# A fused attention and GLU kernel: where its PSUM accumulators lie, when its LayerNorm runs, and how its last sums are added

## The chip, the cores and the metric

The kernel runs on one core of a Trainium2 chip. The core has five engines with their own in-order instruction queues: TensorE (PE, matrix products; loading its weights is shown as PEld), VectorE (DVE), ScalarE (ACT), GpSimd (POOL) and SyncE (SP, which here only issues DMA transfers). ACT and POOL issue DMA transfers too. Products are accumulated in PSUM, a small memory of eight banks that PE writes and DVE and ACT read; everything else lies in SBUF or in DRAM.

The metric is the device time of one execution in microseconds, median over runs of the same kernel. Less is better.

## The reference

The input is one sequence of 2048 tokens with 576 features. Two layers follow each other, each with a residual:

```python
h  = x + A(layernorm(x))     # attention: 32 heads of 18; each token sees 8 keys, 2 apart
h2 = h + B(layernorm(h))     # GLU: (sigmoid(x @ w_gate) * (x @ w_up)) @ w_down, 4608 hidden

# A
qkv = x @ wqkv                                   # [2048, 1728]
idx = pos[:, None] - 2 * arange(8)[None, :]      # the window; negative positions are masked
logits = einsum("bhsd,bhswd->bhsw", q, k[idx]) * 18 ** -0.5
o = einsum("bhsw,bhswd->bhsd", softmax(logits), v[idx]) @ wo
```

All data are fp32.

## The kernel before, in words

**Blocks.** The tokens are split by parity (a window steps by 2, so even tokens see only even ones) and by half, into four blocks of 512 tokens, each of 4 sub-blocks of 128. Each fp32 operand is split into a high part, which ACT rounds to fp32r (L105), and a low part, which DVE makes by subtraction (L106); a product is three matmuls: high by high, low by high, high by low. The last 64 features are packed twice into a fifth chunk (L108 to L110).

**QKV stage.** The 32 heads are four groups of 8. `qkv(b, g, ...)` (L355) makes q, k and v of one block and one group in four tiles of 14 matmuls with 432 columns (L151 to L154), which ACT copies out (L362), and three DMAs of ACT's queue write q, k and v to DRAM (L364 to L368). `ln1` (L327) normalizes a block by sub-blocks: statistics on DVE, the power on POOL, the scaling on ACT for blocks 1 to 3 (L131 to L133), then five transposes on PE (L140, L144) and a split (L105 to L110). `norm` runs a whole `ln1`, `heads` whole QKV products, in the order of L412 to L445. `attention` (L160) loads q and the windows of k and v again (SP) and works almost wholly on DVE (L173 to L207); it is a generator, and `step` lets it go on by a given number of steps after each tile of PE's work, so that it lies beside the matmuls. `att_all` (L376) has the order of its eight runs for blocks 0 and 1. When block 0 is done, `front` projects it, adds the residual, normalizes and transposes it for the MLP.

**MLP.** The 36 hidden tiles of 128 are gone through for the first pair of blocks, then for the second pair. The first 14 tiles of a pair are "std" items, for one block alone (`single`, L597); after that come "pair" items (`pair`, L623), for both blocks together by seven products of sums in place of eight, in three accumulators: b1 takes the products b00, t2, t1 and b11, b2 takes b10, b3 takes t3 and t4. Every product is six matmuls of 512 columns (L562), with two more for the packed rest (L569). Between the products, `between(0)` to `between(6)` let other work in: attention of blocks 2 and 3 in the first pair stage, down projections from a queue. In the second pair's pair stage, tiles 0 to 31 are projected down by seven products as well (`down_seven`, L722), whose results POOL's DMAs add up in DRAM (`hsev`); the last four tiles go by `down_tail` (L708), which adds to sums that `load_tails` (L1024) has loaded back, and writes the output.

**Weights.** One load per item (L516) brings the weights of one hidden tile into one of two buffers, two items ahead; `weights` (L528) splits them at a high priority.

**Order.** The kernel is written in a framework that sets the order on each engine by a simulated time line, from the order of the text and priorities (`high_priority`); each engine then works through its own list in that order, and waits are put in by the framework. `issue_after` holds instructions behind a given one. Memory is given out in pools: tiles of one tag share a number of buffers, and a new tile waits until a buffer is free.

## Time and profile before

| | us |
|---|---|
| time, median of 3 runs (lowest to highest) | 1610.49 (1609.51 to 1611.9) |
| the profiled execution by its own time | 1611.02 |
| its span in the profile | 1609.2 |
| PE busy | 1562.2 (97%) |
| DVE busy | 1253.3 (78%) |
| ACT busy | 881.9 (55%) |
| POOL busy | 191.4 (12%) |

The span runs from the first to the last recorded instruction; the time of the execution holds a little more. "Busy" is the time in which at least one instruction of an engine is on record. A matmul's record (0.39 us for 512 columns) is longer than the distance to the next one, as matmuls overlap, so short gaps between matmuls don't show as idle in full. The granted clock is the share of TensorE's full clock that it was given in a stretch. A row of a group reads: line, engine, operation, output and inputs with their sizes, count, busy us, mean ns of one, and the engine's idle time ahead of them with what ended it. In a row of the timeline, the first two numbers are start and length in us, and the bracket is the idle time ahead and what ended it. In a row of waits the three numbers are us in total, times, and the longest.

### The profile page before, as it was taken

How to read it: one execution, taken by the hardware profiler on the slowest of the kernel's cores; microseconds unless marked ns; L12 is line 12 of the kernel's file. 1: busy time of each engine (PE TensorE's matmuls, PEld its weight loads, DVE VectorE, ACT ScalarE, POOL GpSimd, SP SyncE). 2: the span in 40 equal slices, each digit the busy share in tenths (PEclk: the TensorE clock that was granted, in tenths of full speed). 3: DMA queues.
4: the chain of work that ended last, by engine and by line, in shares of the span. 5: the costliest groups of instructions: out<-in, count | busy, mean ns of one | idle time of the engine just before them, and what ended most of it. 6: DMA issues, size and time to landing. Idle time of an engine off the chain costs nothing.

```text
span 1609.2 us, 22432 instructions
## 1 busy us (share of the span) xinstructions
PE 1562.2 (97%) x8532; PEld 1381.6 (86%) x8532; DVE 1253.3 (78%) x1982; ACT 881.9 (55%) x1565; POOL 191.4 (12%) x230
## 2 busy tenths in 40 slices
PE   7899999999999999999999999999999999999998
PEld 6799988798788888888889987888888888888887
DVE  7989999648999999999635777777767777767755
ACT  6423235534455565555543344677767777667751
POOL 2000010001010010000011100121211221121210
PEclk9899999999999999999999999999999999999999
DMA  7446666654468565666685224699998999989992
GB/s 265 160 150 221 222 236 180 176 184 150 142 165 209 146 168 145 165 166 156 191 249 192 77 88 126 147 185 177 180 173 168 180 190 179 178 164 183 184 192 106
DMA packets 77788, 278.22 MB, mean 173 GB/s; under 512 B 8336, under 2 KB 14224, under 8 KB 76784
## 3 DMA queue, kind: packets, MB, share of 16 engines
q0 software_dynamic: 28944, 111.19, 39.0%
q1 hardware_dynamic: 40304, 143.70, 25.9%
q10 hardware_dynamic: 8432, 21.89, 3.6%
q8 instruction: 67, 1.10, 0.3%
q14 instruction: 41, 0.34, 0.1%
HBM read 145.88 MB, written 133.23 MB: 173 GB/s over the span
## 4 chain that ended last, share of the span: by engine, by line
PE 78%; DVE 12%; ACT 3%; DMA 3%; issue 3%; POOL 0%; SPq 0%; ACTq 0%; DVEq 0%; POOLq 0%
PE b L562 36%; PE dp L733 11%; PE dp L671 11%; PE acc L151 8%; PE b L569 7%; DVE pr L173 2%; DVE pr L199 2%; DVE w L106 1%; DVE lg L176 1%; PE bgp L151 1%; PE b L151 1%; DMA wg<-in_wmlp_dram 1%; DVE pr L204 1%; DVE s L582 1%; PE acc L154 1%
## 5 line engine op out<-in xcount | busy, mean ns | idle before, releaser
L562 PE MATMUL b<-tl,w 128*128 128x512 f32 x1728 | 443.2, 394 | 12.4 <-DVE s L582 6.6
L562 PEld LDWEIGHTS b<-tl,w 128*128 128x128 f32 x1728 | 314.1, 188 | 77.0 <-DVE s L582 6.7
L562 PE MATMUL b<-th,w 128*128 128x512 f32 x1380 | 360.3, 394 | 7.1 <-ACT s L645 5.7
L562 PEld LDWEIGHTS b<-th,w 128*128 128x128 f32 x1380 | 251.8, 188 | 58.8 <-ACT s L645 8.9
L105 ACT ACTIVATE w<-wg 128x640 fp32r<-128x640 f32 (+2 forms) x200 | 118.6, 597 | 168.4 <-PE b L569 108.7
L569 PE MATMUL b<-th,w 128*128 128x512 f32 x576 | 178.8, 390 | 0.0
L106 DVE TENSOR_TENSOR w<-wg,w 128x640 fp32r<-128x640 f32 (+2 forms) x200 | 129.2, 649 | 58.1 <-ACT w L105 55.0
L742 POOL DMA_DIRECT2D h<-ev x128 | 110.8, 868 | 442.8 <-ACT ev L739 428.1
L151 PE MATMUL acc<-qw,th 128*128 128x432 f32 x512 | 156.0, 366 | 0.8 <-ACT th L105 0.8
L739 ACT ACTIVATE ev<-dp 128x576 f32<-128x576 f32 x224 | 141.9, 649 | 24.6 <-PE dp L733 22.4
L569 PEld LDWEIGHTS b<-th,w 128*128 128x128 f32 x576 | 108.1, 188 | 22.9
L671 PE MATMUL dp<-d,h0h 128*128 128x288 f32 x640 | 123.4, 296 | 0.6 <-ACT stage L679 0.6
L671 PE MATMUL dp<-d,h1h 128*128 128x288 f32 x640 | 121.5, 295 | 0.5 <-DVE tail L681 0.5
L106 DVE TENSOR_TENSOR w<-tw,w 128x512 fp32r<-128x512 f32 x116 | 79.5, 686 | 45.4 <-ACT w L105 45.4
L671 PEld LDWEIGHTS dp<-d,h0h 128*128 128x128 f32 x640 | 101.8, 189 | 6.7 <-ACT stage L679 0.9
L671 PEld LDWEIGHTS dp<-d,h1h 128*128 128x128 f32 x640 | 100.6, 188 | 5.5 <-DVE tail L681 0.7
L151 PEld LDWEIGHTS acc<-qw,th 128*128 128x128 f32 x512 | 98.8, 193 | 5.8 <-ACT th L105 1.3
L151 PE MATMUL acc<-qw,tl 128*128 128x432 f32 x256 | 94.5, 369 | 0.4 <-DVE tl L106 0.4
L679 ACT ACTIVATE stage<-dp 128x576 f32<-128x576 f32 x112 | 71.1, 646 | 39.7 <-PE dp L671 39.2
L105 ACT ACTIVATE w<-tw 128x512 fp32r<-128x512 f32 x116 | 73.1, 630 | 30.0 <-PE b L562 23.4
L362 ACT ACTIVATE ev<-acc 128x432 f32<-128x432 f32 x64 | 33.8, 530 | 98.8 <-PE acc L154 98.8
L646 DVE TENSOR_TENSOR s<-s,b 128x512 f32<-128x512 f32 x58 | 39.6, 683 | 59.3 <-ACT s L645 59.3
(268 smaller groups left out, 2933.7 us busy)
## 6 DMA issues: line engine op xcount, KB each, us to landing
h<-ev POOLq DMA_DIRECT2D x96, 576.0 KB, 7.0
wg<-in_wmlp_dram SPq DMA_DIRECT2D x49, 928.0 KB, 5.7
h<-stage POOLq DMA_DIRECT2D x28, 1152.0 KB, 10.2
wg<-in_wmlp_dram SPq DMA_DIRECT2D x36, 640.0 KB, 4.8
kw<-k SPq DMA_DIRECT2D x16, 792.0 KB, 5.3
vw<-v SPq DMA_DIRECT2D x16, 792.0 KB, 4.8
wd<-in_wmlp_dram SPq DMA_DIRECT2D x18, 576.0 KB, 6.4
h<-ev POOLq DMA_DIRECT2D x32, 288.0 KB, 5.9
```

The lines of the kernel that those rows point to most:

```text
L105: act.activation(hi, src, AF.Copy)
L106: splits.append(dve.tensor_tensor(lo, src, f32(hi), ALU.subtract))
L151: pe.matmul(ps[:, :n], a[:, c, js], m[:, c], start=k == 0, stop=False)
L362: act.activation(ev[:, :, j], ps[:, :NQ].rearrange("p (t c) -> p t c", t=3), AF.Copy)
L562: pe.matmul(ps, wt[:, a, k0 + c], xx[:, m + c], start=first and k == 0, stop=k == 5, skip_group_check=True)
L569: pe.matmul(ps, wt[:, a, k0], xx[:, 4], start=False, stop=a == 1, skip_group_check=True)
L646: added[0] = dve.tensor_tensor(s3, s3, b3, ALU.add)
L671: pe.matmul(ps[:, i, :DH2], a[:, js], d[:, m, i * DH2:(i + 1) * DH2], start=k == 0, stop=k == n)
L679: act.activation(hv, ps, AF.Copy)
L733: pe.matmul(ps[:, i, :DH2], a[x][:, js], m[y], start=k in (0, 1, 3) and q == 0, stop=q == 2, skip_group_check=True)
L739: act.activation(hs[:, k % 2], ps[:, :, :DH2], AF.Copy)
L742: pool.dma_start(hsev[:, u, k0:k + 1], hs[:, :k + 1 - k0], accum_op=ALU.add, max_dma_last_dim=8 * D)
```

## The change

Four groups of edits.

- **Pair items:** the three accumulators change places from item to item (`turn`), and ACT copies b3 out right behind the t3 product, to which DVE later adds b1 (before: ACT copied b1 behind t1, and DVE added b3).
- **QKV stage:** `beside` puts the LayerNorm of a block, sub-block by sub-block, behind the tiles of a QKV product of another block. The order of the products and of the attention runs changes: block 0's four attention runs come first. QKV weights, and the two halves of the output weights, share three buffers (before: two, and an extra one). k and v lie in one DRAM tile per group and are written by one DMA; the zero pads likewise. The logits have two buffers.
- **MLP weights:** raw weights have three buffers and are loaded three items ahead; the first item's weights are split into a free operand buffer at the end of the QKV stage (`first_weights`).
- **End:** the stored sums are loaded into tiles of their own, and the second of two is added by an accumulating DMA of POOL. The first group of `down_tail` is copied out by ACT; in the last group DVE adds the stored sums and then the PSUM result. The scratch for the descriptors of POOL's DMAs is set to 8192.

```diff
@@ pads, attention
-            for s in (kscr, vscr):
-                a = s[e][g][0:LP, :]
-                sp.dma_start(..., zero)
+            a = kvscr[g][e]
+            sp.dma_start(..., zero.rearrange("p (t n) -> p t n", t=2))
-        lg = sm.tile([P, NS, W, HG], F32, bufs=1, name="lg")
+        lg = at.tile([P, NS, W, HG], F32, bufs=2, name="lg")
@@ ln1, qkv_w, qkv
-            pri = 2 * HI if b == 0 else HI if b > 1 else 0
+            pri = 2 * HI if b == 0 else HI
+    def qw_tile(name):
+        return saw.tile([P, 2, 5, NQ], F32R, tag="qw", bufs=3, name=name)
-        for t, s in ((1, kscr), (2, vscr)):
-            act.dma_start(s[e][g][r0:r0 + TB, :].rearrange("(p j) c -> p (j c)", p=P),
-                          ev[:, t].rearrange("p j c -> p (j c)"))
+        act.dma_start(kvscr[g][e][:, r0:r0 + TB].rearrange("t (p j) c -> p t (j c)", p=P),
+                      ev[:, 1:3].rearrange("p t j c -> p t (j c)"))
@@ att_all
-        for b, g in ((0, 0), (0, 1), (1, 0), (0, 2), (0, 3), (1, 1), (1, 2), (1, 3)):
+        for b, g in ((0, 0), (0, 1), (0, 2), (0, 3), (1, 0), (1, 1), (1, 2), (1, 3)):
@@ order of the QKV stage
+    def beside(b, xb, order, n):
+        gl = ln1(b, xb)
+        T.append(next(gl))
+        for a, g in order:
+            for _ in qkv(a, g, T[a], w[g]):
+                next(gl, END)
+                step(ag, n)
+        drain(gl)
...
-    heads(((0, 1),), w, 0)
-    norm(1, xb, 0)
+    beside(1, xb, ((0, 1),), 0)
+    w.append(qkv_w(2))
     pads(1)
+    pads(2)
+    heads(((0, 2),), w, 1)
     xb = load_x(2)
-    heads(((1, 0),), w, 1)
-    norm(2, xb, 1)
+    beside(2, xb, ((1, 0),), 2)
     xb = load_x(3)
-    heads(((2, 0),), w, 2)
-    norm(3, xb, 1)
+    beside(3, xb, ((2, 0),), 2)
     heads(((3, 0),), w, 2)
-    w.append(qkv_w(2))
-    pads(2)
-    heads(((1, 1), (0, 2), (2, 1), (3, 1)), w, 2)
     w.append(qkv_w(3))
     pads(3)
+    heads(((0, 3), (1, 1), (2, 1), (3, 1)), w, 2)
     h = load_x(0)
...
+    wos = [None, wo_w(1, wo_tile("wo1"))]
+    heads(((1, 2), (2, 2), (3, 2)), w, 2)
+    wos[0] = wo_w(0, wo_tile("wow"))
@@ weights of the first item, and their loads
+    def first_weights(ws):
+        t = th_tile().rearrange("p a (b n) -> p (a b) n", n=P)
...
+        split(w1[:, 0], w1[:, 1], r[:, 5:10])
+        split(w2[:, 0], w2[:, 1], r[:, 3:5])
+        split(w4[:, 0], w4[:, 1], r[:, 0:3])
     with tc.high_priority(HI):
         drain(fr)
+        first = first_weights(wg)
-        ws = gw.tile([P, WC], F32, bufs=2, name="wg")
+        ws = gr.tile([P, WC], F32, bufs=3, name="wg")
...
-            wc = weights(items[c + 1][0], wg, c + 1 < NF + NSTD)
-        if c + 2 < len(items):
-            wg = load_gu(items[c + 2][2], n=WC if c + 2 < NF + NSTD else GU)
+            wc = weights(items[c + 1][0], raws.pop(0), c + 1 < NF + NSTD)
+        if c + 3 < len(items):
+            raws.append(load_gu(items[c + 3][2], n=WC if c + 3 < NF + NSTD else GU))
@@ pair
-        b1, b2, b3 = b_tile(0), b_tile(1), b_tile(2)
+        b1, b2, b3 = (b_tile(i + turn[0]) for i in range(3))
+        turn[0] += 1
...
         prod(b3, X["s3"], w, "t3", True)
+        with tc.high_priority(HC):
+            act.activation(s3, b3, AF.Copy)
         between(3)
         prod(b1, X["s1"], w, "t1", False)
         rest(b1, X["a11"], w, "u4")
         with tc.high_priority(HC):
-            act.activation(s3, b1, AF.Copy)
-            added[0] = dve.tensor_tensor(s3, s3, b3, ALU.add)
+            added[0] = dve.tensor_tensor(s3, s3, b1, ALU.add)
@@ down_tail
+            if end:
+                with ExitStack() as ties:
+                    for i in over:
+                        ties.enter_context(tc.issue_after(i))
+                    dve.tensor_tensor(hv, hv, tile_j(more[b], j), ALU.add)
-            add_tile(hv, down_tile(seg, b - 2, j), False)
+            add_tile(hv, down_tile(seg, b - 2, j), not end)
@@ load_tails
-        yield from lag(7)
-        for a, m in adds:
-            with tc.issue_after(getattr(added[0], "ins", added[0])):
-                dve.tensor_tensor(a, a, m, ALU.add)
-            yield
+                        if i == 0:
+                            sp.dma_start(more[b][:, h], src)
+                        else:
+                            pool.dma_start(more[b][:, h], src, accum_op=ALU.add,
+                                           max_dma_last_dim=8 * D)
+        yield
@@ kernel
-    nc = _bacc.Bacc("TRN2", target_bir_lowering=False, num_devices=1)
+    nc = _bacc.Bacc("TRN2", target_bir_lowering=False, num_devices=1,
+                    dynamic_dma_scratch_size=8192)
```

`over` holds the last two split instructions of the last item, and each add of the last group: the adds of stored sums are held behind them on DVE.

## The prediction

> **What bounds the kernel now.** The first view is the page's busy table.

> ```profile
> span 1609.2 us, 22432 instructions
> PE 1562.2 (97%) x8532; PEld 1381.6 (86%) x8532; DVE 1253.3 (78%) x1982; ACT 881.9 (55%) x1565; POOL 191.4 (12%) x230
> ```

> TensorE (PE) sets the end. The change neither adds nor removes a matmul, so only time in which PE stands still or runs slowly can be won: 1609.2 - 1562.2 = 47 us of visible idle, and some more, because a matmul's record is longer than the interval to the next one. The second view shows where that time lies: busy time by stretch. The columns are the stretch, its length, busy us (and instructions) of PE, PEld, DVE, ACT, POOL, the granted TensorE clock, the DMA share and GB/s.

> ```profile
> 8.67:36.27 27.60, 27.20 (x132) 25.14 (x133) 21.46 (x78) 19.74 (x41) 6.83 (x12) 1.00 0.71 244
> 36.27:46.00 9.73, 6.72 (x34) 5.94 (x33) 8.65 (x14) 5.32 (x17) 1.33 (x3) 0.82 0.96 365
> 69.50:80.00 10.50, 7.25 (x27) 5.81 (x26) 10.27 (x14) 3.65 (x13) 0.00 (x0) 0.67 0.47 162
> 80.00:187.00 107.00, 107.00 (x548) 102.43 (x547) 96.80 (x105) 30.26 (x63) 0.92 (x1) 1.00 0.56 197
> 187.00:230.00 43.00, 41.73 (x264) 39.64 (x263) 41.58 (x71) 13.07 (x28) 4.77 (x6) 1.00 0.56 188
> 230.00:242.00 12.00, 9.02 (x36) 6.04 (x35) 11.93 (x13) 6.74 (x12) 0.00 (x0) 1.00 0.97 367
> 242.00:297.00 55.00, 54.98 (x292) 47.86 (x291) 49.54 (x66) 29.87 (x49) 3.17 (x3) 1.00 0.61 176
> 297.00:326.00 29.00, 25.54 (x134) 21.76 (x133) 16.36 (x24) 13.28 (x24) 2.75 (x3) 0.94 0.71 216
> 393.00:440.00 47.00, 42.67 (x203) 34.52 (x202) 43.48 (x60) 23.26 (x38) 1.24 (x1) 0.96 0.46 148
> 440.00:778.00 338.00, 330.52 (x1801) 288.00 (x1801) 322.18 (x435) 191.98 (x316) 29.46 (x29) 1.00 0.62 158
> 989.00:1020.00 31.00, 27.32 (x123) 21.32 (x122) 23.16 (x42) 16.79 (x29) 2.85 (x3) 1.00 0.63 157
> 1020.00:1560.00 540.00, 540.00 (x2924) 474.52 (x2924) 386.93 (x673) 385.16 (x680) 109.94 (x127) 1.00 0.92 176
> ```

> Three things are to be seen. From 1020 to 1560 us, the second pair stage, PE is never idle, so nothing can be won there. The losses lie at the two LayerNorms of the QKV stage (36 to 46 and 69.5 to 80 us, with the clock down to 0.82 and 0.67), at the start of the MLP (230 to 242), around 297 to 326, through the first pair stage (393 to 778), and at 989 to 1020. And from 187 to 297 and from 393 to 778 us VectorE (DVE) is about 95% busy with the attention that runs beside the matmuls: there PE can only become faster as far as DVE has room.

> **The change part by part.** The profiled execution took 1611.0 us by its own time, 1.8 us more than its span, and 0.5 us above the median of 1610.49. The sum is made against 1611.0.

> *LayerNorm between QKV tiles.* A full-rate QKV matmul takes 107.00 / 548 = 0.195 us (stretch 80 to 187).

> ```profile
> 36.27 0.60 PE L140 MATMUL mm<-ident,tok 128*128 128x128 f32 x4
> ...
> 36.82 0.60 PE L140 MATMUL mm<-ident,tok 128*128 128x128 f32 x4
> ...
> 41.67 0.86 PE L140 MATMUL mm<-ident,tok 128*128 128x128 f32 x4 [2.21 <-DVE tl L106]
> ```

> Five transposes take 0.55 us (36.27 to 36.82). The stretch from 36.27 holds 20 transposes and 14 QKV matmuls, 4 x 0.55 + 14 x 0.195 = 4.9 us of work in 9.73: 4.8 us are lost, some 3.0 to idleness and 1.8 to the clock. In the stretch from 69.5 at most 27 x 0.195 = 5.3 us of work stand in 10.5: 5.2 lost. Both times PE has emitted all transposes of a block and has nothing else until the first split of the block comes back. After the change, four tiles of another QKV product lie between them, so each split has 14 x 0.195 = 2.7 us of cover. I leave 0.5 us in each place: **4.3 and 4.7 us won**; if the splits are late, at least 0. The third LayerNorm and the output projection idle 43.00 - 41.73 = 1.3 us (187 to 230); block 0's attention is now first in DVE's list, one attention earlier: **0.5**, between 0 and 1.3.

> The cover needs ScalarE (ACT) to keep up.

> ```profile
> L362 ACT ACTIVATE ev<-acc 128x432 f32<-128x432 f32 x10 | 5.2, 524 | 11.9 <-PE acc L154 11.9
> L105 ACT ACTIVATE th<-mm 128x512 fp32r<-128x512 f32 x8 | 4.9, 612 | 1.6 <-PE mm L140 1.6
> L132 ACT ACTIVATE tok<-tok,rstd 128x576 f32<-128x576 f32 x6 | 4.3, 771 | 0.0
> L131 ACT ACTIVATE tok<-h,nm 128x576 f32<-128x576 f32 x4 | 2.8, 766 | 0.0
> L109 ACT ACTIVATE th<-acc 128x128 fp32r<-128x128 f32 x8 | 2.1, 300 | 0.0
> L133 ACT ACTIVATE tok<-tok 128x64 f32<-128x64 f32 x5 | 1.3, 267 | 0.0
> ```

> These groups of ACT (36.27 to 69.5 us; mean ns behind the busy us) give, per tile with its LayerNorm, 524 + 612 + 771 + 766 + 300 + 267 = 3240 ns. PE's turn is 2.73 + 0.55 = 3.28 us. It just fits. The third weight group, now split before block 0's third QKV product, adds to ACT at 8.67 to 36.27, where it is 19.74 of 27.6 us busy; there is room for five splits of 432 columns (each at most the 0.61 of the 512-column split above).

> [...] The granted clock falls here behind a gap of 2.2 us. [...]

> *First MLP weights split early.* In 230 to 242 us 36 matmuls at 0.225 us (1.35 us for six, below) are 8.1 us of work: 3.9 lost.

> ```profile
> 231.66 1.45 PE L562 MATMUL b<-tl,w 128*128 128x512 f32 x4 [1.25 <-ACT w L105]
> 233.75 1.20 PE L562 MATMUL b<-tl,w 128*128 128x512 f32 x4 [0.65 <-DVE w L106]
> ```

> The two waits for split weights go, as the splits now run under the last QKV product: **1.9**, between 0 (DVE is 11.93 of 12 us busy, so the same work may surface later) and 3.9.

> *Third weight buffer; attention's end.* The rows are PE, POOL, PE.

> ```profile
> 300.02 1.63 PE L562 MATMUL b<-tl,w 128*128 128x512 f32 x6 [1.35 <-DVE s L582]
> 307.27 0.75 POOL L210 DMA_DIRECT2D o<-kw  x1 [19.87 <-DVE kw L207]
> 320.85 0.66 PE L140 MATMUL b<-ident,oj 128*128 128x128 f32 x4 [1.65 <-DMA oj<-o]
> ```

> The wait at 300.02 follows a late weight load; loading one item further ahead removes it: **1.4**. But the last attention of block 1 leaves DVE only at 307.27, and PE already waits for its reload at 320.85. If PE comes 4.3 + 4.7 + 0.5 + 1.9 = 11.4 us earlier, DVE must do the same. Between 80 and 297 us DVE idles 10.2 + 1.4 + 0.1 + 5.5 = 17.2 us, much of it behind single waits in its queue, so it will gain part of that. I give back **4**; the ends are 11.4 (DVE gains nothing) and a further gain of 1.65 + 0.06 x 29 = 3.4 (this wait and its clock go too).

> *PSUM accumulators and the third eviction.* In a pair item, b1 took the last product and the next item's first, and product t4 could enter b3 only after ACT had copied b1 (L645) and DVE had added b3 (L646). Afterwards ACT copies b3 before the t1 product, and the next item starts in another accumulator.

> ```profile
> 1003.95 1.52 PE L562 MATMUL b<-tl,w 128*128 128x512 f32 x6
> 1005.30 0.61 PE L569 MATMUL b<-th,w 128*128 128x512 f32 x2
> 1006.61 1.65 PE L562 MATMUL b<-th,w 128*128 128x512 f32 x6 [0.69 <-ACT s L645]
> ```

> Six matmuls take 1.35 us, and t4 starts 1.31 us behind a group that needs 0.45: 0.86 us lost each time no down projection lies between. The weight loads' waits by window, 380 to 790, 985 to 1025 and 1560 to the end:

> ```profile
> PEld b L562 <- DVE s L582: 7.1, 7, 2.3
> PEld b L562 <- ACT s L645: 4.4, 4, 1.1
> PEld b L562 <- DVE s L646: 1.6, 2, 1.4
> ...
> PEld b L562 <- ACT s L645: 3.3, 3, 1.4
> PEld b L562 <- DVE s L651: 1.2, 1, 1.2
> ...
> PEld b L562 <- ACT s L645: 1.1, 1, 1.1
> PEld dp L671 <- DVE tail L681: 0.7, 1, 0.7
> ```

> In the first pair stage 7.1 + 4.4 + 1.6 = 13.1 us hang on these accumulators, plus 0.04 x 47 = 1.9 of clock: 15.0. DVE idles only 3.5 + 15.8 = 19.3 us in these 385, and would be 366 of 370 us busy if all came true. I take **9** (between 4, the waits for ACT alone, and 15). What is late next there is DVE's split of the hidden halves, which the change leaves alone. At 985 to 1025 DVE has room (23.16 of 31): **4** of 4.5, at least 3.

> *The end.* Stored sums are added into one tile by the DMA, and the last but one group of units is evicted by ACT, not added by DVE. L645's 1.1 and the 0.7 go. But these units no longer wait for the loaded sums, move up between the last pair items, and no longer lie between the last product and the last group; that one waits for its hidden split: multiply, ACT, about 0.7 + 0.6 us from DVE's and ACT's 128x512 rows, 1.2 after overlap. DVE gets two adds per unit.

> ```profile
> 1604.80 0.75 DVE L681 TENSOR_TENSOR tail<-tail,dp 128x576 f32<-128x576 f32 x1 [0.84 <-PE dp L671]
> ```

> DVE works 0.75 us per unit and idles 0.84 before it, so the second add of 0.75 fits, just. **0.6**, between -2.4 (both waits are paid) and 1.8. The merged k and v stores (16 ACT issues fewer), the merged pads (8 SP issues fewer), the second logits buffer and the output weights, which now wait for a QKV weight slot and are used only behind the last QKV product, I cost at nothing: they lie on ACT's and SP's queues and under PE's 107 busy us of 80 to 187; uncovered, they would delay attention, which is in the 4 above.

> Sum: 4.3 + 4.7 + 0.5 + 1.9 + 1.4 - 4 + 9 + 4 + 0.6 = 22.4 us. 1611.0 - 22.4 = **1588.6**.

> **The rivals.** *DVE is the bound.* What PE wins up to the reload comes back there in full, the 1.4 with it, and the first pair stage yields only 4: 4 + 4 + 0.6 = 8.6, so 1602.4. For it: the 95% busy stretches; against: 17.2 and 19.3 us idle in them.

> *All covers hold.* Every upper bound: 4.8 + 5.2 + 1.3 + 3.9 + 1.4 + 3.4 + 15 + 4.5 + 1.8 = 41.3, so 1569.7. For it: the second pair of blocks' attention is used late and may slip; against: DVE's queue is in order, and PE's splits stand in it.

> *LayerNorm is late at every turn: slower.* The transposes of three blocks now stand in PE's queue at 12 places, each in front of a QKV tile. If ACT's 3.24 us per turn stretch beyond PE's 3.28, each place waits. The whole sum then stands against 12 new waits: from 22.4 / 12 = 1.9 us per place on the gain is gone, and at the 2.2 us of today's wait on tl L106 it is 1611.0 - 22.4 + 26.4 = 1615. Against it: one late turn gives the next ones time.

> [...]

> *The order stays.* Engines follow the planner's simulated order, so the text's order may change little on PE: 1608 to 1614.

> **How the numbers follow.** Forecast 52% (own range 1580 to 1597), DVE bound 22% (1597 to 1607), all covers 13% (1569 to 1580), late LayerNorm 6%, POOL stall 1%, order stays 6%. A change within 0.2% (3.2 us) can't be told from none. Faster 0.87, same 0.06, slower 0.07. 1572 to 1606 leaves out 13% above, 2% at the upper edge of the DVE case and some 3% below.

> **What would show it.** Right: in the stretches 36 to 46 and 69 to 80 the clock stays at 1.00 and PE's waits for tl L106 are gone; waits for L645 and L646 vanish from PE's list, those for L582 shrink; DVE rises over 96% in the first pair stage. Wrong: new waits of the transposes on tok L133 or L135, a longer wait on oj, waits on hidden splits in place of L582, or clock dips elsewhere.

## The result and the profile after

| | before | after |
|---|---|---|
| time, median (lowest to highest), us | 1610.82 (4 runs) | 1584.03 (1582.09 to 1586.38; 4 runs) |
| ratio after / before, 95% interval | | 0.9835 (0.9819 to 0.9851) |
| the profiled execution, its span, us | 1611.02, 1609.2 | 1582.11, 1580.3 |

The kernel became 26.8 us faster. The forecast was 1588.6 with a range of 1572 to 1606, so the sign and nearly the size were right. The experiments below show that several terms of the sum were not.

The busy table of the kernel after, and the first row of its chain of work:

```profile
span 1580.3 us, 22467 instructions
PE 1548.5 (98%) x8532; PEld 1377.6 (87%) x8532; DVE 1257.2 (80%) x1979; ACT 879.8 (56%) x1573; POOL 192.4 (12%) x233
PE 87%; DVE 5%; issue 3%; DMA 2%; ACT 2%; POOL 0%; ACTq 0%; SPq 0%; DVEq 0%; POOLq 0%
```

PE's visible idle fell from 47.0 to 1580.3 - 1548.5 = 31.8 us. The stretches, with the columns that the prediction explains:

```profile
36.27:46.00 9.73, 8.57 (x49) 7.86 (x48) 9.21 (x26) 7.27 (x20) 3.04 (x4) 1.00 1.01 379
69.50:80.00 10.50, 10.35 (x58) 9.61 (x58) 10.24 (x13) 5.10 (x16) 0.00 (x0) 1.00 0.20 75
230.00:242.00 12.00, 6.55 (x22) 5.05 (x23) 11.97 (x12) 4.25 (x8) 0.00 (x0) 0.72 0.79 293
297.00:326.00 29.00, 28.07 (x159) 24.47 (x157) 14.86 (x25) 14.70 (x27) 3.92 (x4) 1.00 0.88 274
440.00:778.00 338.00, 337.60 (x1863) 298.44 (x1863) 319.38 (x433) 196.76 (x326) 28.58 (x27) 1.00 0.66 170
```

The clock at the two LayerNorms is back at 1.00 in this profile, and in the first pair stage PE is idle for 0.4 us where it was for 7.5. At 230 to 242 it became worse: 22 matmuls in place of 36. PE's longest waits of the whole run now (us in total, times, longest):

```profile
PE mm L141 <- DVE tok L136: 8.2, 1, 8.2
PE b L576 <- DVE w L106: 5.1, 1, 5.1
PE b L576 <- DVE s L598: 3.0, 5, 1.8
PE bgp L152 <- DVE hj L245: 1.9, 1, 1.9
PE mm L141 <- ACT tok L133: 1.7, 2, 1.3
PE mm L141 <- ACT th L109: 1.2, 1, 1.2
```

(The first is the wait for the first data. Line numbers moved: L562 is now L576, L569 L583, L582 L598, L671 L694, L681 L704.)

Because busy time hides short gaps (the record of a matmul of 512 columns lasts 0.39 us, the next one starts after 0.227), the two traces are compared by a **loss**: for each matmul, the time to the start of the next one, less the median of that time for matmuls of the same width (227 ns for 512 columns, 196 for 432, 132 for 288, 109 for 128, the same to 1 ns in the traces of before and after). It holds idle time and slow pitch alike. All losses of the kernel before sum to 67.9 us, of the kernel after to 39.7.

| stretch of each kernel's own time, us | before | after | won | forecast |
|---|---|---|---|---|
| 20 to 60, first LayerNorm between tiles | 5.9 | 1.4 | 4.5 | 4.3 |
| 60 to 92, second | 6.6 | 4.2 | 2.4 | 4.7 |
| 180 to 220, third, output projection | 2.2 | 2.3 | -0.1 | 0.5 |
| 220 to 240, start of the MLP | 4.0 | 7.5 | -3.5 | 1.9 |
| 240 to 440, std items, reload of attention | 15.9 | 8.9 | 6.9 | 1.4 - 4 |
| 440 to 790, first pair stage | 14.0 | 2.3 | 11.7 | 9 |
| 790 to 985, second pair's std items | 3.2 | 3.2 | 0.0 | - |
| 985 to 1020, start of the second pair stage | 5.5 | 0.2 | 5.2 | 4 |
| 1520 to the end | 3.3 | 2.3 | 0.9 | 0.6 |

### The profile page after: what moved, and what is told of

It is laid out like the page before. It is cut to its first block, busy times and chain, and to the rows that moved or that the text cites. A ratio compares the mean times of both kernels' runs of the same rounds, so it can differ in the third digit from the quotient of the medians.

```text
span 1580.3 us, 22467 instructions
## 1 busy us (share of the span) xinstructions
PE 1548.5 (98%) x8532; PEld 1377.6 (87%) x8532; DVE 1257.2 (80%) x1979; ACT 879.8 (56%) x1573; POOL 192.4 (12%) x233
## 3 DMA queue, kind: packets, MB, share of 16 engines
q1 hardware_dynamic: 39360, 141.93, 26.4%
## 4 chain that ended last, share of the span: by engine, by line
PE 87%; DVE 5%; issue 3%; DMA 2%; ACT 2%; POOL 0%; ACTq 0%; SPq 0%; DVEq 0%; POOLq 0%
PE b L576 42%; PE dp L694 14%; PE dp L766 11%; PE acc L152 8%; PE b L583 8%; PE bgp L152 1%; PE b L152 1%; DMA oj<-o 1%; PE acc L154 1%; PE acc L155 1%; DVE pr L174 1%; DVE w L106 1%; DMA ws<-in_wqkv_dram 1%; DVE lg L177 0%; DVE pr L200 0%
## 5 line engine op out<-in xcount | busy, mean ns | idle before, releaser
L576 PE MATMUL b<-tl,w 128*128 128x512 f32 x1716 | 454.3, 393 | 9.1 <-DVE w L106 5.1
L576 PEld LDWEIGHTS b<-tl,w 128*128 128x128 f32 x1716 | 310.7, 188 | 65.3 <-DVE w L106 5.8
L576 PE MATMUL b<-th,w 128*128 128x512 f32 x1368 | 357.2, 392 | 0.8 <-DVE s L672 0.6
L576 PEld LDWEIGHTS b<-th,w 128*128 128x128 f32 x1368 | 251.3, 188 | 48.7 <-DVE s L672 1.1
L772 ACT ACTIVATE ev<-dp 128x576 f32<-128x576 f32 x224 | 145.8, 651 | 114.8 <-PE dp L766 89.6
L583 PE MATMUL b<-th,w 128*128 128x512 f32 x572 | 179.7, 390 | 0.0
L105 ACT ACTIVATE w<-wg 128x640 fp32r<-128x640 f32 (+2 forms) x197 | 117.0, 596 | 93.2 <-PE b L583 60.0
L106 DVE TENSOR_TENSOR w<-wg,w 128x640 fp32r<-128x640 f32 (+2 forms) x197 | 127.4, 649 | 50.2 <-ACT w L105 49.9
L583 PEld LDWEIGHTS b<-th,w 128*128 128x128 f32 x572 | 107.1, 188 | 21.5
L694 PE MATMUL dp<-d,h1h 128*128 128x288 f32 x640 | 123.0, 295 | 0.0
L694 PE MATMUL dp<-d,h0h 128*128 128x288 f32 x640 | 122.5, 295 | 0.3 <-DVE tail L704 0.3
L106 DVE TENSOR_TENSOR w<-tw,w 128x512 fp32r<-128x512 f32 x116 | 79.5, 686 | 38.0 <-ACT w L105 37.9
L694 PEld LDWEIGHTS dp<-d,h0h 128*128 128x128 f32 x640 | 101.5, 188 | 6.3 <-DVE tail L704 0.6
L694 PEld LDWEIGHTS dp<-d,h1h 128*128 128x128 f32 x640 | 101.4, 188 | 5.4
L105 ACT ACTIVATE w<-tw 128x512 fp32r<-128x512 f32 x116 | 73.2, 631 | 53.7 <-PE b L576 41.5
L672 DVE TENSOR_TENSOR s<-s,b 128x512 f32<-128x512 f32 x58 | 39.6, 683 | 62.3 <-PE b L583 62.2
## 6 DMA issues: line engine op xcount, KB each, us to landing
h<-stage POOLq DMA_DIRECT2D x28, 1152.0 KB, 11.4
```

What stands on the lines that cost most here:

```text
L105: act.activation(hi, src, AF.Copy)
L106: splits.append(dve.tensor_tensor(lo, src, f32(hi), ALU.subtract))
L576: pe.matmul(ps, wt[:, a, k0 + c], xx[:, m + c], start=first and k == 0, stop=k == 5, skip_group_check=True)
L583: pe.matmul(ps, wt[:, a, k0], xx[:, 4], start=False, stop=a == 1, skip_group_check=True)
L672: added[0] = dve.tensor_tensor(s2, s2, b3, ALU.add)
L694: pe.matmul(ps[:, i, :DH2], a[:, js], d[:, m, i * DH2:(i + 1) * DH2], start=k == 0, stop=k == n)
```

## The experiments

All times below are medians of several runs beside runs of the kernel before on the same chip; where two changed kernels are compared, their ratios to the kernel before are, with 1% taken as 16.1 us.

### The accumulators: undone, and alone

`u_acc` is the kernel after with both accumulator edits undone; `u_turn` and `u_s3` undo one each; `a_acc` is the kernel before with both edits alone.

```diff
 u_acc, u_turn:
-        b1, b2, b3 = (b_tile(i + turn[0]) for i in range(3))
+        b1, b2, b3 = (b_tile(i) for i in range(3))
 u_acc, u_s3:
-        with tc.high_priority(HC):                        # behind t3
-            act.activation(s3, b3, AF.Copy)
...
         with tc.high_priority(HC):                        # behind t1
-            added[0] = dve.tensor_tensor(s3, s3, b1, ALU.add)
+            act.activation(s3, b1, AF.Copy)
+            added[0] = dve.tensor_tensor(s3, s3, b3, ALU.add)
```

> The changed kernel, with the accumulators of a pair item in fixed places again and the third eviction as it was (copy of the third product, then the add). Theory of separate joints: the whole of what the stretches 393 to 790 and 985 to 1025 won (about 15 us) goes, and the waits on the copy and the add of the third eviction are back in PE's list: 1597 to 1601. Rival, VectorE as the bound: the first pair stage yields only 4 whatever the accumulators do, so undoing them costs at most 4 to 8: 1588 to 1592. Third: part of the 12 us in the pair stage came from elsewhere (second logits buffer, LayerNorm's order); then 1589 to 1596 and the loss of the pair stage comes back only in part.

Measured: 1612.1, ratio 1.0016 (1.0003 to 1.0029). Undoing these two edits takes back 0.0181 x 1610 = 29 us, more than the whole gain and more than any of the three expectations. Its losses against the kernel after: 15.4 us more at 440 to 790, 6.1 at 790 to 985, 4.8 at 985 to 1020, 5.0 at the end. The first and third are the places that the forecast had (17.8 and 5.0 of loss, 14.0 and 5.5 in the kernel before); the other two were on no one's list.

> The changed kernel with the accumulators of a pair item in fixed places; the third eviction keeps its new order. After the run with both undone (27 us lost, of them some 15 in the first pair stage, 6 at the output projection at 830, 5 at 1010, 5 at the end): if the turn carries most, because the next item's first product then waits for the last product's split, 1600 to 1607, with waits on s L598-like multiplies in the first pair stage. If the order of the third eviction carries most: 1586 to 1591. If the two are one joint (each needs the other): both single undoings cost over 15.

> The changed kernel with the third eviction in its old order (copy of the t1 product, add of b3) and the places still changing. If the third eviction carries most: 1598 to 1607, with waits of the t4 product on the copy and the add. If the turn carries most: 1585 to 1590.

Measured: `u_turn` 1637.08, ratio 1.0167 (1.0151 to 1.0182), so 53 us lost; `u_s3` 1593.74, ratio 0.9895 (0.9879 to 0.9912), 10 us lost. Neither time lies in one of the expected ranges. The turn carries the gain: without the new third eviction the first pair stage loses 2.5 us, much as with it (2.3), and most of the 10 us come from 790 to 985 (7.4 more; see the next section). With the new eviction but fixed places the stage loses 39.6. So without the turn the new eviction does harm: `u_turn` is 24 us slower than `u_acc`, which has neither (1.0167 against 1.0016). PE's weight loads there, 380 to 790 us, in `u_turn` and then in the kernel after:

```profile
PEld b L576 <- DVE s L598: 26.5, 13, 3.4
PEld b L576 <- DVE s L667: 3.7, 5, 2.3
```

```profile
PEld b L576 <- DVE s L598: 4.1, 4, 2.2
PEld b L576 <- ACT tl L105: 1.4, 2, 1.1
```

One of the thirteen in the timeline of `u_turn`, on DVE and on PE:

```profile
457.94 2.55 DVE L177 TENSOR_REDUCE lg<-pr 128x128 f32<-128x2304 f32 x1
460.40 0.68 DVE L106 TENSOR_TENSOR w<-tw,w 128x512 fp32r<-128x512 f32 x1
461.00 0.82 DVE L106 TENSOR_TENSOR w<-wg,w 128x640 fp32r<-128x640 f32 x1
461.73 0.68 DVE L598 TENSOR_TENSOR s<-s 128x512 f32<-128x512 f32 x1
462.33 0.68 DVE L598 TENSOR_TENSOR s<-s,b 128x512 f32<-128x512 f32 x1
```

```profile
463.07 1.66 PE L576 MATMUL b<-tl,w 128*128 128x512 f32 x6 [2.34 <-DVE s L598]
```

The multiply that clears an item's last accumulator (L598) stands behind a 2.55 us reduction of the attention and two weight splits; with fixed places the next item's product needs that very accumulator. `u_acc` has the same fixed places and only 7.0 us of this wait, as its order on DVE is another; what set the worse order in `u_turn` stays open.

> The kernel before with the two accumulator edits alone. Forecast by the joints: 9 + 4 of the sum, as measured in the whole change some 11.5 + 5 = 16: 1593 to 1597 against a before of 1610. Rival (what the undoing showed): the accumulators are worth 27 on their own, since orders further on hang on them: 1582 to 1585. Rival, VectorE as the bound: without the other edits it gives 4 to 8: 1602 to 1606.

Measured: 1607.55, ratio 0.9988 (0.9976 to 1.0001): 2 us, not told apart from none. None of the three expectations held. The losses say why: against the kernel before, `a_acc` wins 9.9 us at 440 to 790 and 4.5 at 985 to 1020, the 9 and 4 of the forecast almost to the number, and loses 5.8 at 790 to 985, 4.8 at the end and 2.8 in between (the last not looked into). Two waits that were not there before took the gain.

### The wait at the second output projection

In `a_acc` PE stands 5.39 us at 832 us. Its rows, and those of DVE, ACT and POOL ahead of it:

```profile
837.68 0.61 PE L151 MATMUL b<-wow,th 128*128 128x288 f32 x1 [5.39 <-DVE hj L244]
```

```profile
836.44 0.82 DVE L106 TENSOR_TENSOR w<-wg,w 128x640 fp32r<-128x640 f32 x1 [9.46 <-ACT w L105]
837.18 0.45 DVE L244 TENSOR_TENSOR hj<-hj,b 128x288 f32<-128x288 f32 x1
```

```profile
834.70 0.92 ACTq L878 DMA_DIRECT2D h<-stage  x2
835.67 1.15 ACT L105 ACTIVATE w<-wg 128x640 fp32r<-128x640 f32 x2 [10.53 <-POOL stage L876]
```

```profile
832.65 2.02 POOL L876 MEMSET stage<- 128x2304 f32 x1 [15.24 <-DMA h<-stage]
```

Read from below: POOL zeroes a staging tile once the store of its last sums has landed. ACT is to store these zeros (L878) and stands 10.53 us in front of the two DMAs; its weight copies wait behind them, DVE's weight split waits for the copy, the addition of the residual (L244) stands behind the split, and PE needs that addition to free a PSUM bank. Each engine waits for another, and PE stands. The kernel after has the same stall of ACT (10.5 us, from 816.6 to 827.1), and PE's wait of 1.9 on hj L245 comes from it.

`b_z` and `a_accz` are the kernel after and `a_acc` with these two stores issued by POOL itself. On every engine all other instructions stay in their order.

```diff
-                act.dma_start(hsev[:, u, 1:6:2],
+                pool.dma_start(hsev[:, u, 1:6:2],
```

> The changed kernel with the two stores of zeros under the second output projection (line 908) issued by POOL, which makes the zeros, instead of ScalarE; every other instruction stays in its order on its engine. Theory: ScalarE stands some 10 us in front of these stores, for POOL's memset, which waits for the store of the last sums to land; its weight copies, VectorE behind them and TensorE behind VectorE follow. Then the 2.0 us loss at 828 goes: 1581 to 1583 against 1584, ScalarE's wait of 10.5 us at 827 gone. Rival, the projection is late by VectorE's own work: the loss at 828 stays, 1584.

> The kernel before with the two accumulator edits alone, as a_acc (1607.55), and the zeros stored by POOL. If the gain of the accumulators was lost at the output projection to ScalarE's wait for these stores, the 5.5 us at 832 come back: 1601 to 1603. Rival: the loss moves on to the next wait (the end, where loaded sums are late): 1605 to 1608.

Measured: `a_accz` 1599.66, ratio 0.9934 (0.9921 to 0.9948) against 0.9988 (0.9976 to 1.0001): 8.7 us faster by one moved issue, more than expected, and the loss at 790 to 985 falls from 9.0 to 2.0. `b_z` 1581.46, ratio 0.9822 (0.9809 to 0.9836); the loss at 790 to 985 falls from 3.2 to 1.1, which is the 2 us expected, though the two kernels' intervals overlap. Its median is the lowest here. ACT's waits from 815 to 840 us in `a_acc`, then in `a_accz`:

```profile
ACT w L105 <- POOL stage L876: 10.5, 1, 10.5
ACT stage L682 <- PE dp L674: 4.0, 2, 2.6
```

```profile
ACT w L105 <- DMA wg<-in_wmlp_dram: 4.2, 2, 2.4
ACT h1h L105 <- PE dp L674: 4.0, 1, 4.0
```

The loss of `u_acc` and `u_s3` at 790 to 985 reads as the same chain. POOL, ACT, DVE and PE in `u_s3`:

```profile
820.20 2.02 POOL L905 MEMSET stage<- 128x2304 f32 x1 [13.48 <-DMA h<-stage]
```

```profile
822.25 1.54 ACTq L907 DMA_DIRECT2D h<-stage  x2
823.84 0.60 ACT L624 ACTIVATE s<-b 128x512 f32<-128x512 f32 x1 [11.44 <-issue]
```

```profile
825.09 0.83 DVE L106 TENSOR_TENSOR w<-wg,w 128x640 fp32r<-128x640 f32 x1 [13.66 <-ACT w L105]
825.95 0.29 DVE L110 TENSOR_TENSOR th<-bgp,th 64x128 fp32r<-64x128 f32 x1
```

```profile
826.30 0.61 PE L152 MATMUL bgp<-tl,th 128*128 128x288 f32 x1 [5.99 <-DVE th L110]
```

So 6.1 of the 29 us of `u_acc` and 7.4 of the 10 us of `u_s3` stand behind these stores. Neither was run with the zeros stored by POOL; what the third eviction is worth without the stall stays open.

### The end

`u_end` is the kernel after with the end of before (sums loaded by SP, added by DVE, four adds of PSUM results).

```diff
-                with ExitStack() as ties:
...
-                    dve.tensor_tensor(hv, hv, tile_j(more[b], j), ALU.add)
-            add_tile(hv, down_tile(seg, b - 2, j), not end)
+            add_tile(hv, down_tile(seg, b - 2, j), False)
...
+                sp.dma_start(hs[:, h], hsev[:, :, k].rearrange("p u i n -> p u (i n)"))
...
+                dve.tensor_tensor(a, a, m, ALU.add)
```

> The changed kernel with the old end (sums loaded and added by VectorE, the last but one group added too). Theory from a_acc, where the loaded sums stood in VectorE's queue 4.1 us late and PE lost 4.2: with changing places the old end costs about 4: 1587 to 1589. By the forecast's 0.6: 1584 to 1585.

Measured: 1589.62, ratio 0.9875 (0.9861 to 0.9888), 6.4 us slower than the kernel after. DVE and PE in `u_end`:

```profile
1558.80 1.36 DVE L1072 TENSOR_TENSOR tail<-tail,more 128x1152 f32<-128x1152 f32 x1 [6.47 <-DMA tail<-h]
1560.08 0.68 DVE L672 TENSOR_TENSOR s<-s,b 128x512 f32<-128x512 f32 x1
1560.68 1.41 DVE L704 TENSOR_TENSOR tail<-tail,dp 128x576 f32<-128x576 f32 x2
```

```profile
1561.57 0.82 PE L694 MATMUL dp<-d,h0h 128*128 128x288 f32 x2 [6.41 <-DVE tail L704]
```

The loaded sums come 6.5 us late for a faster PE, and DVE's queue stands in front of them; in the kernel before the same add ran without a wait. `a_acc` had 4.0 us of it.

### LayerNorm, raw weights, first weights, logits

```diff
 u_ln:
             for _ in qkv(a, g, T[a], w[g]):
-                next(gl, END)
                 step(ag, n)
 u_raw:
-        ws = gr.tile([P, WC], F32, bufs=3, name="wg")
+        ws = gr.tile([P, WC], F32, bufs=2, name="wg")
...
-        if c + 3 < len(items):
+        if c + 2 < len(items):
 u_first:
-        first = first_weights(wg)
...
-        wc = first, d
+        wc = weights("std", wg, True)
 u_lg:
-        lg = at.tile([P, NS, W, HG], F32, bufs=2, name="lg")
+        lg = at.tile([P, NS, W, HG], F32, bufs=1, name="lg")
```

> The changed kernel with the LayerNorm of a block behind the other block's QKV product instead of between its tiles; nothing else. Separate joints: 4.5 us at the first and 2.4 at the second place come back, with waits on tl L106 and a lower granted clock there: 1590 to 1592. Rival, VectorE as the bound up to attention's reload: what PE loses early it gets back as shorter waits on oj and on item 1's weights (5.1 and 1.2 us are there to get back): 1584 to 1586.

Measured: 1591.79, ratio 0.9896 (0.9878 to 0.9914): 9.8 us. That is what was expected if the edit's gain stands by itself. It lost 9.6 us at 20 to 92, another 1.4 at 92 to 180 and 2.9 at 220 to 300, and got 4.3 back at 300 to 440. PE's waits at 55 to 95 us have the two on DVE's splits again, and a new one:

```profile
PE mm L141 <- ACT tok L133: 5.0, 1, 5.0
PE mm L141 <- DVE tl L106: 4.6, 2, 2.5
```

> The changed kernel with two raw weight buffers and the load two items ahead instead of three. Separate joints: the waits of the std items for split weights (1.4 at one place before, some 3 to 5 in the stage in all) come back and nothing else: 1585.5 to 1589. Rival, the splits stand behind attention on VectorE whatever the load does: 1583 to 1585.

Measured: 1592.53, ratio 0.9893 (0.9876 to 0.9909): 9.3 us, more than either expectation. It is the load that is late, not the split. ACT and PE in `u_raw`:

```profile
315.02 1.15 ACT L105 ACTIVATE w<-wg 128x640 fp32r<-128x640 f32 x2 [5.67 <-DMA wg<-in_wmlp_dram]
```

```profile
315.81 2.64 PE L576 MATMUL b<-tl,w 128*128 128x512 f32 x6 [3.57 <-ACT w L105]
```

Another 4.2 us of its loss came at 790 to 985, where ACT stands 9.6 us in front of the zeros' stores.

> The changed kernel with item 0's weights split at the start of the MLP, as before the change. If the early split is worth what was forecast (1.9 us): 1586, with waits of PE on w L105 and w L106 of item 0 at 230. Rival: the early split only moved the wait to item 1 (the 5.06 us at 236), as the queue of VectorE holds the same work: 1582 to 1585, and the sum of the waits between 228 and 242 unchanged.

> The changed kernel with one logits buffer. Costed at nothing in the forecast: 1582 to 1586. Rival: the attention on VectorE in the first pair stage kept pace only by the second buffer: 1588 to 1598, with the loss at 440 to 790 and at 830.

Measured: `u_first` 1583.38, ratio 0.9838 (0.9824 to 0.9853), and `u_lg` 1583.5, ratio 0.9835 (0.982 to 0.985): neither edit is worth anything that can be measured. In `u_first` the wait of 5.1 us for item 1's weights stands as in the kernel after, and a wait for item 0's is back:

```profile
226.46 2.37 PE L575 MATMUL b<-tl,w 128*128 128x512 f32 x8 [1.25 <-ACT w L105]
240.73 2.07 PE L575 MATMUL b<-tl,w 128*128 128x512 f32 x4 [5.06 <-DVE w L106]
```

### Three repairs at once

`b_zas` adds to `b_z` that item 1's raw weights are loaded by ACT's queue, and that block 1's second QKV product stands ahead of block 0's fourth.

```diff
-    heads(((0, 3), (1, 1), (2, 1), (3, 1)), w, 2)
+    heads(((1, 1), (0, 3), (2, 1), (3, 1)), w, 2)
-        wg2 = load_gu(1, pool)
+        wg2 = load_gu(1, act)
```

> The zeros stored by POOL, item 1's raw weights loaded by ScalarE's queue instead of POOL's, and block 1's second QKV product ahead of block 0's fourth. If the three losses of the changed kernel (2.0 at 828, 5.1 at 236, 1.2 at 90) each go by themselves: 1576 to 1580. As the runs so far showed that one shifted order moves waits elsewhere: 1580 to 1588 with the waits at 90 and 236 gone and others in their place.

Measured: 1591.84, ratio 0.9887 (0.9874 to 0.9901), slower than both expectations. The wait at 90 is gone and the one at 236 fell from 5.1 to 3.0, but 300 to 440 loses 12.2 us more than in `b_z`: a weight copy of ACT waits 8.12 us for its load at 337, and PE 4.22 behind it. SP issues that load at 320.4, right behind the reloads for the output projection, and it lands 16.8 us later. The reloads are issued from 315.6 on, in `b_z` from 303.9 on, as they wait for the attention of block 1; that points to the changed order of the QKV products, but the two edits were not run apart.

## Why the prediction was right, and where it was not

**The bound.** Right: no engine but PE set the end, and all that was won were gaps and slow pitch in the places that the stretches showed.

**LayerNorm.** 4.3 against 4.5 at the first place, with clock and wait as forecast. At the second, 4.7 against 2.4: the step that failed is "It just fits". ACT did block 3's scalings in one batch ahead of the first transposes, and PE waited 1.3 and 0.4 us for tok L133; a third 1.2 us at 90 is the fourth weight group, which waits for a buffer of the three. Undoing the edit costs 9.8 us, near the 9.5 of the three terms: 11 us at the QKV stage, of which a part came back as shorter waits later on.

**The clock.** The prediction let the time of the slow clock, 1.8 us at the first LayerNorm, go with the gaps. They went together: in the profile of the kernel after, the stretches 36 to 46 and 69.5 to 80 came back to 1.00 from 0.82 and 0.67, as PE's longest waits there shrank from 2.21 and 2.22 us on tl L106 to 1.16 on th L109 and, just ahead of the second stretch, 1.32 on tok L133. At the second place this was in part luck: `b_z` has the same wait of 1.32 us on tok L133, and the clock of 67.5 to 72 us is 0.74 there, where the kernel after has 1.00. What the traces show of the clock behind gaps stands in the last section.

**First weights.** 1.9 forecast; 3.5 lost in that stretch, and undoing the edit costs or wins nothing. The two waits for item 0's weights did go, but PE waits 5.06 us for those of item 1. DVE and PE in the kernel after:

```profile
230.16 2.55 DVE L177 TENSOR_REDUCE lg<-pr 128x128 f32<-128x2304 f32 x1
232.74 2.63 DVE L174 TENSOR_TENSOR pr<-kw,q 128x1152 f32<-128x1152 f32 x2
235.29 2.36 DVE L106 TENSOR_TENSOR w<-wg,w 128x640 fp32r<-128x640 f32 x4
```

```profile
236.16 2.08 PE L576 MATMUL b<-tl,w 128*128 128x512 f32 x4 [5.06 <-DVE w L106]
```

Item 1's splits stand behind two attention steps of 5.2 us. `u_first` has this wait as well, so the early split did not bring it; which other edit put the attention steps there was not tested. Beside `u_first`, the early split wins 2.9 us of loss at 220 to 300 us (7.7 against 10.6) and gives 2.9 back at 300 to 440 (8.7 against 5.8). So the stretch fell below the lower bound of 0 for another reason, and the edit itself is worth nothing in the end, as the bound had allowed.

**Third raw buffer and the give-back.** 1.4 - 4 forecast, 6.9 won. The 1.4 sized the wait as it stood in the trace of before; for a PE that comes earlier the load itself would be late, and undoing the buffer costs 9.3, of which 4.2 stand behind the zeros' stores. The give-back did not come: the last attention of block 1 was stored by POOL at 298.90, before at 307.27, 8.4 of the 11.4 us asked for, and the wait on the reload is 0.9 where it was 1.65. So DVE could use part of the 17.2 us that it idled before.

**Pair stage.** 9 forecast of 4 to 15, 11.7 won, and 4 of 4.5 at 985 where 5.2 came. The mechanism held (waits for the copy and the add are gone, the multiply's shrank from 7.1 to 4.1), but not the reason for taking 9. DVE was not pressed to 96%: it is 319.38 of 338 us busy, 94.5%. The attention has room behind it. Its last output was stored at 777.5 and read at 806.7 in the kernel before, 783.0 and 793.3 in the kernel after: the slack between shrank from 29 to 10 us, and PE did not wait for it. The rival "DVE is the bound" fell for the same reason.

**The end.** 0.6 forecast, 0.9 won, and yet the edit is worth 6.4. The term was reckoned against the end as the kernel before showed it; with the accumulators changed, that end loses 4.8 (`a_acc`) to 6.7 us (`u_end`) more than its 3.3 in the kernel before.

**The sum.** 22.4 forecast, 26.8 measured. That it came so near rests on errors that cancel: too much at the second LayerNorm and the first weights (7.7 together), too little at the raw buffer, give-back and pair stage (13.4). And a sum of terms is the wrong form: undone one by one, accumulators, LayerNorm, raw buffer and end cost 29 + 9.8 + 9.3 + 6.4 = 54.5 us, twice the gain, while the accumulators alone win 2. Each edit wins time at its place and brings PE sooner to the next late transfer; the other edits take those out of its way. The prediction named such returns up to the reload alone. An unchanged order did not show, and the late LayerNorm only in the waits on tok L133. Nor did the stall of POOL, which had 1%: from 1020 to 1520 us, where most of its accumulating stores run, PE's loss is 4.0 us where it was 4.1. What the size of the descriptor scratch does by itself no run shows.

## What to carry to other kernels

A wait's length in the trace of before is the price of an edit only for the PE that comes as late as before: for each transfer or copy behind a gap that goes, read how much slack it has left (here PE then waited 3.6, 5.4 and 6.4 us for a load, a store and the stored sums), and name it as the next wait. A DMA issue that waited for another engine held up all that stood behind it on its own queue (ACT's weight copies for 10.5 us, in `a_acc` as in the kernel after); let the engine that makes the data issue it (one such move was worth 8.7 us where PE had become early, 2 where it had not). In a kernel whose order is planned as a whole, undo edits one at a time in the finished kernel as well as trying them alone: the two answers, 29 and 2 us here, are both true. A stall elsewhere can be part of either price, as the zeros' stores were here.

## What the runs showed of the hardware

```profile
67.50:72.00 4.50, 3.81 (x22) 3.05 (x23) 4.36 (x5) 4.50 (x13) 0.00 (x0) 1.00 0.49 180
```

```profile
67.50:72.00 4.50, 3.93 (x18) 3.06 (x19) 4.36 (x5) 4.50 (x13) 0.00 (x0) 0.74 0.48 180
```

The same 4.5 us hold 22 matmuls at a clock of 1.00, or 18 at 0.74. In two more runs the clock of this stretch is 1.00 (`u_lg`) and 0.76 (`u_acc`). What decides between the two was not shown. It may also be why the kernel after took 1582.1 us twice, at a mean clock of 0.998, and near 1586 twice, at 0.997 and 0.995; that was not tested.
